# A fused attention, gated-convolution MLP and Fourier-mixing kernel: two of batch 0's eight MLP units in split numbers, eight opening products of zeros, another planner setting and order

## Chip, cores and metric

The kernel runs on one core of one Trainium2 chip. The metric is the device time of one execution in microseconds. The kernel before took 733.38 us (median of 3 runs, 733.23 to 734.42); the execution whose trace is read here took 731.59 us.

## What is computed

```python
# q, k, v: (4 batches, 8 heads, 576 tokens, 64); d_model 512
def _attn_ref(q, k, v):            # heads 0-3: window of 32; heads 4-7: window 128, every 4th token
    scores = np.where(masks[None], scale * (q @ k.T), -1e9)
    attn = softmax(scores)
    return attn @ v
def _moe_ref(x, w_in, conv_w, w_out):          # 512 -> 1024 -> 512
    h = np.maximum(x @ w_in, 0.0)
    gate = sigmoid(conv3(h, conv_w))           # along the tokens
    return (h * gate) @ w_out
def _moe2_ref(x, w_ch1, w_ch2):                # 512 -> 2048 -> 512
    u = x + real(fft(fft(x, axis=1), axis=2))
    un = layernorm(u)
    return u + np.maximum(un @ w_ch1, 0.0) @ w_ch2
```

The three weight matrices arrive as 64-bit floats and are turned into 32-bit numbers on the chip.

## The kernel before

**Numbers.** Most products are made with split numbers: an fp32 value is cut into a high part (rounded by writing it as fp32r) and a low part (value minus high part), and `mm3` (L291) issues three fp32r products, high by high, high by low and low by high. A plain `mm` on fp32 operands is one product that the trace shows as two matmul records.

**Stages.** (1) Attention: 14 steps a batch (`tick`, L648), each with score products, a maximum over partitions on GpSimd, an exponential on ScalarE, value products and transposes. The result of a batch is its tokens, transposed: for batch 0 in plain fp32 (`x_first`, L552), for the others split (`x_even` for batch 2, `x_odd` for 1 and 3). (2) The gated MLP, eight units of 128 hidden columns a batch (`mlp1`, L1395): `m1` (L738) makes a unit's hidden columns in two halves of 290 tokens, four products over d_model each, then the convolution and gate on ScalarE and VectorE; `m2` (L773) multiplies by the second matrix with `mm3`. (3) The Fourier transform as products with tables. (4) Layer norm and the second MLP in sets of 6 token tiles; there the first product uses seven products of 256-column blocks in place of eight (`weights7`, `sums7`, `tokens7`, L1175 to L1218, make the block sums on VectorE).

**Weights of the first MLP.** `Weights.convert` (L573) loads a raw 64-bit block, and `narrow` (L599) makes fp32 of it in three VectorE operations. For the second matrix `split` (L586) copies the high part and subtracts for the low part. For the first matrix the split is put off: batch 0 uses the plain fp32 weight. `narrow` writes it to one of three buffers (`ways`), a DMA copies it into its place, batch 0's `m1` multiplies it with `x_first` by plain `mm`, and `W1.later(f)` (L591, called for batch 1 at L1400) makes the split there: a copy for the high part and a subtraction that overwrites the plain weight.

**Order.** Nothing is issued in the order in which it is written. Every operation is a `Work` with estimated costs on the engines that can do it, a due time and its dependencies. `Plan.order` (L318) simulates the engines with these costs and always takes the most urgent ready work; the result is a fixed instruction stream for each engine. A transfer is planned to land 2.0 us after its bytes have gone over the bus (L408). Before that, each entry of `NUDGES` (L193) is a random seed that shifts the due times in one stretch of the plan by up to 8 us. Where the plan finds TensorE idle for over 0.4 us it fills the gap with small products (`busy_with`, L1301).

**Opening.** TensorE begins with 11 products of zeros (L1321) while the first operands arrive. The first transfers (L1337 to L1344) go over two queues, SP's and ScalarE's; the mask's middle part, `maskt[:, 384:768]`, is the last of them, on SP. `tick` 0 needs the mask's first part, `tick` 1 the middle part, and the dilated ticks the last part.

Of the kernel before, what the change touches and what calls it, by code (L numbers as in the profile page):

```python
# [45 lines left out]
T0 = 42.0  # L46
ROOT = (False, True, True)
PER = 68.0
T4 = T0 + 4 * PER
WHEN = {"dft": ((T4 - 65, 3.4), (T4 - 31, 3.4), (T4 + 40, 2.0), (T4 + 65, 2.5)), "first": (T4 - 2, 5.4),  # L50
        "rest": T4 + 44, "lead": 8.0, "six": 15.5}
# [136 lines left out]
class Work:  # L188
# [1 line left out]

NUDGES = (72935, 65452, 92148, 75732, 27922, 34960, 38538, 92972, 84579, 18235, 76564, 47731,  # L193
          74478, 2462, 75030, 82671, 84525, 15307, 83166, 68938, 50299, 5828, 74961, 19298,
          26748, 40657, 30353, 18642, 13928, 90295, 84765, 10537,)


LAT = {"PE": 0.25, "DVE": 0.12, "ACT": 0.15, "POOL": 0.2, "SP": 0.0, "NO": 0.0}
# [5 lines left out]
class Plan:  # L204
# [113 lines left out]
    def order(self):  # L318
        W = self.works
        for w in W:  # L320
            w.succ, w.left, w.ready, w.start = [], len(w.deps), 0.0, None
        for w in W:
            for d in w.deps:
                W[d].succ.append(w.id)
        self.urgency()
        for seed in NUDGES:
            rng = random.Random(seed)
            a = rng.uniform(0, 560)
            z = a + rng.uniform(4, 50)
            amp = rng.choice((1, 2, 4, 8))  # L330
            for w in W:
                if a < w.key < z:
                    w.key += rng.uniform(-amp, amp)
        self.urgency()
        free = dict.fromkeys(("PE", "DVE", "ACT", "POOL", "SP", "NO"), 0.0)
        can = {e: {} for e in free}
        bus, drift, last = 0.0, 0.0, 0.0
        out = []
        seen = dict.fromkeys(self.uses, (0, 0.0))

        def fill(t0, t1):


            free_at = []
            for tile_, uses in self.uses.items():
                i, end = seen[tile_]
                while i < len(uses) and uses[i][0].start is not None:
                    x = uses[i][0]
                    i, end = i + 1, max(end, x.start + x.where[x.eng])
                seen[tile_] = i, end  # L350
                if 0 < i < len(uses) and uses[i][1]:
                    free_at.append((end, len(free_at), tile_))
            end, _, tile_ = min(free_at, default=(t1, 0, None))
            n = int((t1 - max(t0, end) - 0.25) / 0.12)
            return self.busy_with(tile_, max(t0, end), n) if n > 0 else []

        def can_wait(w, end):
            return w.key < 1e8 and end < w.key + min(w.where.values()) + drift

        def offer(w):  # L360
            for e in w.where:
                can[e][w.id] = w
        for w in W:
            if not w.left:
                offer(w)
        while any(can.values()):
            best = None
            for e, c in can.items():
                if c:
                    t = max(free[e], min(w.ready for w in c.values()))  # L370
                    if best is None or t < best[0]:
                        best = t, e
            t, e = best
            pick = None

            wait = WAIT.get(e, 0.0)
            for w in sorted((w for w in can[e].values() if w.ready <= t + wait + 1e-9), key=lambda w: w.key):
                late = False
                for e2, us in w.where.items():
                    if e2 != e:  # L380
                        queue = sum(x.where[e2] for x in can[e2].values()
                                    if x.key < w.key and x.ready <= t and len(x.where) == 1)
                        if max(free[e2], t) + queue + us < t + w.where[e] - 1e-9 and not (
                                us < w.where[e] and can_wait(w, t + w.where[e] + 0.5)):
                            late = True
                if not late:
                    pick = w
                    break
            if pick is None:

                free[e] = min([f for x, f in free.items() if f > t + 1e-9] + [t + 0.3])
                continue
            w = pick
            for x in w.where:
                del can[x][w.id]
            t = max(t, w.ready)
            w.start, w.eng = t, e
            if e == "PE":
                if 8.0 < t and t - last > 0.4 and self.busy_with:
                    out += fill(last, t)  # L400
                last = t + w.where[e]
                drift += 0.1 * (t - w.key - drift)
            end = t + w.where[e]
            free[e] = end
            if w.bytes:
                begin = max(bus, end)
                bus = begin + w.bytes / (300e3 if begin < 60.0 else 280e3)
                end = bus + 2.0  # L408
            out.append(w)
            for s in w.succ:  # L410
                x = W[s]
                lat = 0.0 if w.bytes else LAT[e] if e not in x.where else 0.0
                x.ready = max(x.ready, end + lat)
                x.left -= 1
                if not x.left:
                    offer(x)
        assert all(w.start is not None for w in W), [w.id for w in W if w.start is None][:5]
        return out
# [51 lines left out]
def tile_kernel(ctx: ExitStack, tc: tile.TileContext, forms, qt_in, qt_first, ktp, ktd, vtp, vtd, wm1, wm2, conv_w,  # L470
# [22 lines left out]
    def dve(op_, us, key=None, **kw):  # L493
        P.run({"DVE": us}, op_, key, **kw)
# [68 lines left out]
    class Weights:  # L563
# [9 lines left out]
        def convert(self, where, raw, load=True):  # L573
            _, i, f = self.todo[self.at]
            self.at += 1
            w = self.tiles[i, f] = where
            if load:
                dma(raw, self.src[f, :, i])
            if self.late and not i:
                way = ways()  # L580
                self.narrow(raw, way)
                dma(w[:, 0].bitcast(F32), way)
            else:
                self.split(w, raw)
# [153 lines left out]
    def m1(b, f, h_banks, at):  # L738
# [8 lines left out]
        for half in range(2):  # L747
            o = of("h", h_banks)[:, :HS + 2]
            sl = slice(286 * half, 286 * half + HS + 2)
            with P.products(at + 4.3 * half):  # L750
                for c in range(4):
                    wsl = slice(128 * c, 128 * c + 128)
                    if b:
                        mm3(o, w[:, 0, wsl], w[:, 1, wsl], xT[b][:, c, 0, sl], xT[b][:, c, 1, sl], c == 0, c == 3)
                    else:
                        mm(o, w[:, 0, wsl].bitcast(F32), x_first[:, c, sl], c == 0, c == 3)
            P.run({"ACT": 0.41}, "activation", out=hp[:, HW + 2:] if half else hp[:, 1:HW],
                  in_=o[:, HS + 1:0:-1] if half else o, func=AF.Relu, scale=0.5)
# [416 lines left out]
    def weights7(j, raw, stage):  # L1175
# [8 lines left out]
        s1, s2, s3, s4 = (o[:, k] for o in odd for k in (k0, k1))  # L1184
        for o, a, b, op in ((s1, x[1][:, k0], x[1][:, k1], ALU.add), (s2, s1, x[0][:, k0], ALU.subtract),
                            (s3, x[0][:, k0], x[1][:, k0], ALU.subtract), (s4, x[0][:, k1], s2, ALU.subtract)):
            dve("tensor_tensor", on_dve(256), out=o, in0=a, in1=b, op=op)
        for k, a in ((0, x[0]), (2, x[1][:, k1]), (3, odd[0]), (5, odd[1])):
            n = a.n() // 256
            o, a = stage[:, k:k + n], a.rearrange("p (i n) -> p i n", i=n)  # L1190
# [10 lines left out]
    def sums7(j, raw, place_):  # L1201
# [6 lines left out]
        x21, x22, s3, s4 = (b[:, 256 * i:256 * i + 256] for i in range(4))  # L1208
        for o, x, y, op in ((s1, x21, x22, ALU.add), (s2, s1, x11, ALU.subtract),
                            (s3, x11, x21, ALU.subtract), (s4, x12, s2, ALU.subtract)):  # L1210
            dve("tensor_tensor", on_dve(256), out=o, in0=x, in1=y, op=op)
        for i, r in enumerate((a, b)):
            o = place_[:, 2 * i:2 * i + 2]
            v = r[:, 512:1024].rearrange("p (i n) -> p i n", i=2)
# [3 lines left out]
    def tokens7(s, place7):  # L1218
# [6 lines left out]
                load_un(place7[name][:, :, :, 128 * i:128 * i + 128], k, cs)  # L1225

        def tt(o, a, b, op=ALU.subtract):
            dve("tensor_tensor", on_dve(o.n()), out=o, in0=a, in1=b, op=op)

        def split(v, a):  # L1230
            copy(v[:, 0], a, ("ACT", "POOL"))
# [86 lines left out]
    dve("memset", 0.3, key=-98, out=idle)  # L1318
    zeros = idle.bitcast(BF16)[:, 0:512]
    with P.products(-97):  # L1320
        for _ in range(11):  # L1321
            mm(bank[7], zeros[:, 0:128], zeros, True, True)
    P.run({"POOL": 7.0}, "partition_all_reduce", out_ap=tiny, in_ap=tiny, channels=32,
          reduce_op=bass_isa.ReduceOp.max, key=-100)
# [13 lines left out]
    first(KT[0][:, 0:224], ktp[0, :, 0:224])  # L1338
    first(ident16, ident16_in, "ACT")
    first(QT[0][:, :, 0:192], qt_first)  # L1340
    first(KT[0][:, 224:608], ktp[0, :, 224:608])
    for h, queue in ((0, "SP"), (1, "ACT")):
        first(QT[0][h:128:2, h, 192:], qt_in[0, h, :, 192:], queue)
    first(maskt[:, 384:768], mask[:, 384:768])  # L1344
    P.key = loads[0] + 1
    kq_load(1)
    P.key += 1
# [47 lines left out]
    def mlp1(b, f0, f1, h_banks):  # L1395
        step = PER / NF1
        for f in range(f0, f1):
            at = T0 + PER * b + step * f
            if b == 1:
                W1.later(f)  # L1400
            m1(b, f, h_banks, at)
            m2(b, f, at + 2 * step)

# [207 lines left out]
```

## Time and profile before

| | |
|---|---|
| median of 3 runs | 733.38 us |
| profiled execution | 731.59 us |
| its span, first to last instruction | 729.7 us |
| TensorE matmul busy | 720.5 us |
| TensorE weight loads busy | 634.8 us |
| VectorE busy | 550.3 us |
| ScalarE busy | 341.8 us |
| GpSimd busy | 163.4 us |

Times in the rows below are microseconds from the span's start. PE is TensorE's matmuls, PEld its weight loads, DVE VectorE, ACT ScalarE, POOL GpSimd, SPq and ACTq the issue of DMAs on SyncE's and ScalarE's queues. A name such as `pb<-y,wf` is output from inputs: `pb` a PSUM bank, `wf` a weight place, `y` the storage in which `x_first` lies, `x` split tokens, `hid` the gated hidden values, `sm` an attention tile. A matmul's own duration holds its latency, which overlaps with the next; what a product costs is the distance from its start to the next one's.

### The profile page before, as it was taken

To read this page: it belongs to the slowest core of one execution; us is meant where nothing else is said; L and a number is where in the kernel's file an instruction comes from. 1 tells how busy PE (TensorE), PEld (TensorE's weight loads), DVE (VectorE), ACT (ScalarE), POOL (GpSimd) and SP (SyncE) were. 2 spreads that over 40 slices of the span, in tenths; PEclk is the share of its full clock that TensorE was granted. 3 is DMA by queue.
4 is the path that set the end of the run, shared out by engine and by line. 5 is a ranking of instruction groups with operands and counts; after the bars stand their busy time and mean duration, and the time that the engine had idled before them with its cause. 6 is when DMAs were issued, how large, how long until landed. Compare 5 with 4: busy or idle time off the path is not lost.

```text
span 729.7 us, 11759 instructions
## 1 busy us (share of the span) xinstructions
PE 720.5 (99%) x4135; PEld 634.8 (87%) x4135; DVE 550.3 (75%) x1119; ACT 341.8 (47%) x882; POOL 163.4 (22%) x181
## 2 busy tenths in 40 slices
PE   8999999999999999999999999999999999999998
PEld 6888889998998999888888788898888898888896
DVE  5999999899988689989886986776788548224223
ACT  4877767665876654663343424332233314222211
POOL 6845546353465123201100000000100000000000
PEclk9999999999999999999999999999999999999999
DMA  8967535115321836688877642045467799447202
GB/s 269 322 198 220 184 118 168 57 59 179 104 82 29 316 117 202 198 285 284 275 254 240 198 107 67 30 144 156 119 216 251 294 360 331 119 116 239 79 1 87
DMA packets 76750, 129.02 MB, mean 177 GB/s; under 512 B 7754, under 2 KB 36810, under 8 KB 76052
## 3 DMA queue, kind: packets, MB, share of 16 engines
q1 hardware_dynamic: 75892, 125.37, 53.2%
q0 software_dynamic: 432, 2.67, 1.0%
q8 instruction: 33, 0.54, 0.3%
q10 hardware_dynamic: 368, 0.23, 0.1%
q14 instruction: 25, 0.20, 0.1%
HBM read 90.21 MB, written 35.94 MB: 173 GB/s over the span
## 4 chain that ended last, share of the span: by engine, by line
PE 84%; DVE 7%; DMA 5%; POOL 1%; ACT 1%; SPq 1%; issue 1%; DVEq 0%; POOLq 0%; ACTq 0%
PE pb L274 84%; DVE rows L261 2%; DVE win L261 1%; DMA raw<-in_wm_dram 1%; DVE sm L261 1%; DMA work<-ud 1%; DMA maskt<-in_mask_dram 1%; SPq L307 1%; DVE work L261 1%; DMA wf<-y 1%; POOL mx L261 1%; DMA yd<-y 1%; DMA x<-nd 0%; DVE raw L261 0%; DVE hid L261 0%
## 5 line engine op out<-in xcount | busy, mean ns | idle before, releaser
L274 PE MATMUL pb<-wf,hid 128*128 128x512 f32 x870 | 230.6, 399 | 0.1
L274 PEld LDWEIGHTS pb<-wf,hid 128*128 128x128 f32 x870 | 157.1, 188 | 26.5 <-DVE hid L261 0.7
L261 POOL PARTITION_ALL_REDUCE mx<-sm x56 | 82.9, 1504 | 50.2 <-DVE sm L261 26.4
L274 PE MATMUL pb<-wf,wc 128*128 128x384 f32 (+1 forms) x414 | 85.6, 343 | 0.5 <-DVE work L261 0.5
L274 PE MATMUL pb<-x,wf 128*128 128x290 f32 x576 | 85.7, 300 | 0.0
L274 PEld LDWEIGHTS pb<-x,wf 128*128 128x128 f32 x576 | 80.4, 189 | 1.8
L274 PEld LDWEIGHTS pb<-wf,wc 128*128 128x128 f32 x414 | 74.1, 188 | 6.8 <-DVE work L261 0.8
L261 DVE TENSOR_TENSOR work<-pb,work 128x384 f32<-128x384 f32 x48 | 26.7, 556 | 66.7 <-ACT work L261 35.0
L261 DVE SCALAR_TENSOR_TENSOR rows<-rows,convw 128x578 f32<-128x578 f32 x64 | 57.6, 900 | 2.4 <-ACT rows L261 1.6
L261 ACT COPY work<-pb 128x384 f32<-128x384 f32 x48 | 23.0, 479 | 77.5 <-PE pb L274 77.5
L274 PE MATMUL pb<-wf 128*128 128x512 f32 x216 | 55.3, 393 | 0.0
L274 PEld LDWEIGHTS pb<-wf 128*128 128x128 f32 x216 | 40.1, 188 | 6.5
L274 PEld LDWEIGHTS pb<-VT,sm 104*72 104x72 f32 (+1 forms) x448 | 40.0, 153 | 4.8 <-ACT sm L261 1.2
L274 PE MATMUL pb<-VT,sm 104*72 104x65 f32 (+1 forms) x448 | 41.2, 235 | 1.3 <-ACT sm L261 0.7
L691 ACT ACTIVATE xb<-pb,rs 72x64 f32<-72x64 f32 (+1 forms) x176 | 39.7, 305 | 5.4 <-DVE rs L261 5.0
L274 PE MATMUL pb<-QT,KT 128*104 128x144 f32 (+1 forms) x224 | 40.9, 305 | 0.0
L274 PE MATMUL pb<-wf,wf 128*128 128x512 f32 (+1 forms) x162 | 39.8, 386 | 0.0
L261 ACT ACTIVATE rows<-pb 128x290 f32<-128x290 f32 (+1 forms) x64 | 26.3, 413 | 21.9 <-PE pb L274 21.6
L274 PEld LDWEIGHTS pb<-QT,KT 128*104 128x104 f32 (+1 forms) x224 | 33.4, 178 | 3.3 <-issue 1.2
L261 ACT ACTIVATE hid<-pb 128x512 fp32r<-128x512 f32 (+1 forms) x32 | 18.2, 570 | 36.4 <-PE pb L274 36.4
L274 PEld LDWEIGHTS pb<-wf,wf 128*128 128x128 f32 x162 | 30.0, 188 | 6.0 <-ACT y L261 0.4
L274 PE MATMUL pb<-y,wf 128*128 128x290 f32 x128 | 34.3, 410 | 0.0
(198 smaller groups left out, 1279.8 us busy)
## 6 DMA issues: line engine op xcount, KB each, us to landing
raw<-in_wm_dram SPq DMA_DIRECT2D x42, 512.0 KB, 4.6
wc<-cd SPq DMA_DIRECT2D x56, 256.0 KB, 3.4
cd<-wc SPq DMA_DIRECT2D x4, 1792.0 KB, 10.3
rows<-ud SPq DMA_DIRECT2D x20, 256.0 KB, 3.0
yd<-y SPq DMA_DIRECT2D x18, 256.0 KB, 4.4
y<-yd SPq DMA_DIRECT2D x18, 256.0 KB, 4.6
ud<-y SPq DMA_DIRECT2D x18, 256.0 KB, 4.2
wf<-nd SPq DMA_DIRECT2D x18, 256.0 KB, 6.1
```

The lines of the kernel that those rows point to most:

```text
L261: getattr(self.engines[eng], name)(**a)
L274: getattr(self.engines["PE"], name)(*[v.real() for v in a], **kw)
L307: self.engines[eng].dma_start(out=out.real() if outs else out, in_=in_.real() if ins else in_)
L691: nc.scalar.mul(out=x[:, i], in_=p[:, i], mul=r[:, i:i + 1])
```

## The change

- `WHOLE = 6`: the units 6 and 7 of the first matrix are split when they are converted (`split`, in place, no `ways` buffer, no DMA copy), and their `W1.later` in batch 1 goes. Batch 0's `m1` for these two units uses `mm3`, and before unit 6 its tokens are split into `x_even`: four copies and four subtractions of 128x576.
- 8 products of zeros in place of 11.
- The mask's middle part is issued earlier, on ScalarE's queue, ahead of the rest of the first keys.
- The plan's numbers: a transfer that begins after 200 us lands 3.5 us after its bytes rather than 2.0; the block sums cost 1.2 times and the token sums 1.1 times as much as before.
- `NUDGES`: 27 of the 32 seeds stay, 26 are new, so the order of the whole kernel is another.

```diff
+WHOLE = 6
+SURE = 200.0
-NUDGES = (72935, 65452, ..., 84765, 10537,)                    # 32 seeds
+NUDGES = (72935, 65452, ..., 46324, 2076,)                     # 53 seeds
...
-                end = bus + 2.0
+                end = bus + (2.0 if begin < SURE else 3.5)
...
-            if self.late and not i:
+            if self.late and not i and f < WHOLE:
                 way = ways()
                 self.narrow(raw, way)
                 dma(w[:, 0].bitcast(F32), way)
...
-                    if b:
+                    if b or f >= WHOLE:
                         mm3(o, w[:, 0, wsl], w[:, 1, wsl], xT[b][:, c, 0, sl], xT[b][:, c, 1, sl], c == 0, c == 3)
                     else:
                         mm(o, w[:, 0, wsl].bitcast(F32), x_first[:, c, sl], c == 0, c == 3)
...
-            dve("tensor_tensor", on_dve(256), out=o, in0=a, in1=b, op=op)
+            dve("tensor_tensor", 1.2 * on_dve(256), out=o, in0=a, in1=b, op=op)
...
-            dve("tensor_tensor", on_dve(o.n()), out=o, in0=a, in1=b, op=op)
+            dve("tensor_tensor", 1.1 * on_dve(o.n()), out=o, in0=a, in1=b, op=op)
...
-        for _ in range(11):
+        for _ in range(8):
             mm(bank[7], zeros[:, 0:128], zeros, True, True)
...
     first(QT[0][:, :, 0:192], qt_first)
+    first(maskt[:, 384:768], mask[:, 384:768], "ACT")
     first(KT[0][:, 224:608], ktp[0, :, 224:608])
     for h, queue in ((0, "SP"), (1, "ACT")):
         first(QT[0][h:128:2, h, 192:], qt_in[0, h, :, 192:], queue)
-    first(maskt[:, 384:768], mask[:, 384:768])
...
-            if b == 1:
+            if b == 1 and f < WHOLE:
                 W1.later(f)
+            if b == 0 and f == WHOLE:
+                for c in range(4):
+                    copy(x_even[:, c, 0], x_first[:, c], ("ACT", "POOL"))
+                    lo_of(x_even[:, c, 1], x_first[:, c], x_even[:, c, 0])
```

## Rows read from the trace of the kernel before

**Rows 1.** The page's first part: each engine's busy time, share of span, instructions.

```profile
PE 720.5 (99%) x4135; PEld 634.8 (87%) x4135; DVE 550.3 (75%) x1119; ACT 341.8 (47%) x882; POOL 163.4 (22%) x181
```

**Rows 2.** Waits of PE over the whole span: total, times, longest.

```profile
PE pb L274 <- DMA maskt<-in_mask_dram: 1.1, 2, 0.6
PE pb L274 <- ACT work L261: 0.8, 1, 0.8
PE pb L274 <- ACT sm L261: 0.7, 1, 0.7
PE pb L274 <- DVE work L261: 0.5, 1, 0.5
PE pb L274 <- ACT rs L261: 0.5, 1, 0.5
```

**Rows 3.** Busy time by stretch: length, then each engine's, clock, DMA share, GB/s.

```profile
41.00:100.00 59.00, 58.10 (x342) 47.74 (x341) 57.76 (x102) 42.91 (x134) 30.55 (x32) 1.00 0.58 184
100.00:150.00 50.00, 50.00 (x364) 46.71 (x363) 45.81 (x86) 35.46 (x110) 26.32 (x29) 1.00 0.35 106
...
200.00:250.00 50.00, 49.67 (x352) 45.53 (x351) 40.04 (x79) 34.58 (x106) 23.89 (x27) 1.00 0.41 138
```

**Rows 4.** Timeline of PE, batches 0 and 1: start, length, work, count.

```profile
40.14 2.14 PE L274 MATMUL pb<-y,wf 128*128 128x290 f32 x8
42.12 0.81 PE L274 MATMUL pb<-VT,sm 128*96 128x65 f32 x8
...
83.27 2.12 PE L274 MATMUL pb<-y,wf 128*128 128x290 f32 x8
...
97.77 2.17 PE L274 MATMUL pb<-y,wf 128*128 128x290 f32 x8
...
113.15 1.90 PE L274 MATMUL pb<-x,wf 128*128 128x290 f32 x12
114.89 0.34 PE L274 MATMUL pb<-ident,xb 96*128 96x96 f32 x2
```

**Rows 5.** Timeline of all engines and queues, the first 16 us.

```profile
0.73 0.41 ACTq L307 DMA_DIRECT2D maskt<-in_mask_dram  x1
...
1.37 4.78 PE L274 MATMUL pb<-sm 128*128 128x512 bf16 x11 [1.37 <-DVE sm L254]
...
5.98 0.33 PE L274 MATMUL pb<-maskt,ident 128*128 128x384 bf16 x1
...
7.53 0.32 PE L274 MATMUL pb<-maskt,ident 128*128 128x384 bf16 x1 [0.57 <-DMA maskt<-in_mask_dram]
...
8.81 0.43 SPq L307 DMA_DIRECT2D maskt<-in_mask_dram  x1
...
9.23 7.04 POOL L261 PARTITION_ALL_REDUCE mx<-sm  x5 [0.22 <-ACT sm L261]
```

**Rows 6.** The chain that ended last, in order of time: two transfers after 200 us.

```profile
393.15 5.78 DMA work<-ud
...
532.67 6.48 DMA raw<-in_wm_dram
```

**Rows 7.** Instruction groups by shape, PE: the plan's filling products.

```profile
L1309 PE MATMUL pb<-ident 128*128 128x256 bf16 x10 | 1.4, 274 | 0.0
```

**Rows 8.** Timeline of DVE, POOL and PE between 80 and 107 us.

```profile
80.68 0.69 DVE L261 TENSOR_TENSOR wf<-raw,wf 128x512 fp32r<-128x512 f32 x1
...
86.77 0.76 DVE L261 TENSOR_TENSOR hid<-rows,hid 128x576 fp32r<-128x576 f32 x1 [0.56 <-POOL hid L261]
...
94.12 1.92 POOL L261 PARTITION_ALL_REDUCE mx<-sm  x1
94.68 1.31 DVE L261 TENSOR_TENSOR wf<-raw,wf 128x512 fp32r<-128x512 f32 x1
...
96.12 0.53 PE L274 MATMUL pb<-wf,hid 128*128 128x512 f32 x1
...
106.27 0.36 DVE L261 TENSOR_TENSOR x<-pb,x 128x192 fp32r<-128x192 f32 x1 [0.45 <-ACT x L261]
```

More of the change, by code (lines that the diff above doesn't have):

```diff
@@ L189 @@
     __slots__ = ("where", "fn", "deps", "key", "bytes", "after", "start", "eng", "left", "ready", "succ", "id")
-NUDGES = (72935, 65452, 92148, 75732, 27922, 34960, 38538, 92972, 84579, 18235, 76564, 47731,
-          74478, 2462, 75030, 82671, 84525, 15307, 83166, 68938, 50299, 5828, 74961, 19298,
-          26748, 40657, 30353, 18642, 13928, 90295, 84765, 10537,)
+NUDGES = (72935, 65452, 92148, 75732, 27922, 34960, 38538, 84579, 92863, 47731, 74478, 2462,
[4 rows of a table added]
 LAT = {"PE": 0.25, "DVE": 0.12, "ACT": 0.15, "POOL": 0.2, "SP": 0.0, "NO": 0.0}
@@ L1210, in sums7 @@
                             (s3, x11, x21, ALU.subtract), (s4, x12, s2, ALU.subtract)):
-            dve("tensor_tensor", on_dve(256), out=o, in0=x, in1=y, op=op)
+            dve("tensor_tensor", 1.2 * on_dve(256), out=o, in0=x, in1=y, op=op)
         for i, r in enumerate((a, b)):
```

4 rows, old and new, of the table NUDGES are left out of this document.

## The prediction

> **What bounds the kernel now.** I read first the engines' busy time [rows 1], then who PE waits for [rows 2], then the busy time by stretch [rows 3], and last the timelines of the places that the change touches [rows 4, 5, 8] and the chain of waits [rows 6].
>
> PE is busy for 720.5 of 729.7 us [rows 1]. The reader should see in that line how little is to be had: of the 9.2 us without a product, 1.4 lie before the first one [rows 5], 4.1 are five kinds of waits that add up to 1.1 + 0.8 + 0.7 + 0.5 + 0.5 plus a few of 0.5 and less [rows 2], and the 3.7 that are left lie outside these rows. So only three things can shorten the kernel: less work on PE, an earlier first useful product, and fewer waits. One more place is hidden in "busy": the plan itself put ten small products into gaps, 1.4 us of busy time with nothing to compute [rows 7].
>
> The second thing to see is DVE. Over the whole span it is at 75%, which looks harmless, but that average mixes stretches: from 41 to 100 us, while batch 0 runs through its MLP, DVE is busy for 57.76 of 59 us, from 100 to 150 for 45.81 of 50, and only after 200 does it have a fifth of its time free [rows 3]. In that first stretch two engines are full at once, so whatever is added to DVE there matters.
>
> **The change part by part.**
>
> *Units 6 and 7 by split numbers: PE.* One half of a unit in plain fp32 (four products, eight records) starts at 40.14, and what follows starts at 42.12: 1.98 us. The same half in split numbers (twelve products) takes from 113.15 to 114.89: 1.74 us [rows 4]. Two units have four halves, so 4 x 0.24 = 0.96 us less on an engine with no slack. I take -1.0, with 0.1 us a half for the neighbour that comes after: -0.6 to -1.4. All of it counts, since PE does nothing else meanwhile.
>
> The Trainium skill, page "FP8 and Floating Point Precision", section TensorE Precision Notes, says that true fp32 makes four passes through the array. Three passes in place of four would save a quarter of 1.98, or 2.0 us in all as an estimate from that page; the rows show about half of it, and the rows decide.
>
> *The same units: DVE, ACT, POOL, DMA.* The split of batch 0's tokens adds four subtractions of 128x576, as the one that makes `hid`: 0.76 us each [rows 8], 3.0 us. It also adds four copies of that size on ACT or POOL, which are busy for 42.91 and 30.55 of 59 us there [rows 3] and hide them. The two weight subtractions are moved, not added: from batch 1 to before unit 6, 0.69 us each [rows 8], 1.4 us. So by the time unit 6 starts, at 83.27, and unit 7 ends, near 100 [rows 4], DVE has 4.4 us more to do, and 1.24 us were idle there. Two DMA issues on SP and their copies go, and with them the way through a buffer; neither SP nor the transfers hold anything there (DMA share 0.58 [rows 3]), so I cost that at nothing. If DVE can't be relieved the price is several microseconds: the low part of one weight is written from 94.68 to 95.99 and the product that reads it starts at 96.12 [rows 8], no margin at all. What relieves it: copies out of PSUM and the scaling of attention results which the planner may give to DVE or to ACT, the room on DVE after 100 us, and the 1 us that the opening moves everything forward. I take +0.4, between 0 and 4.4.
>
> *A new wait.* `x_even` was free until batch 2 wrote it; now batch 2's writes wait for batch 0's last product. That ends near 99.8 (97.77 + 2.0 [rows 4]) and the first low part of batch 2 is written at 106.27 [rows 8]. Behind it on ACT and DVE would stand the batch-1 work; with 6 us of distance it costs nothing.
>
> *The opening.* The eleven products of zeros begin at 1.37 and the first useful product starts at 5.98, right behind the last of them, with no wait of its own [rows 5]. They are 4.61/11 = 0.42 us apart, so eight end 1.26 us earlier. The useful product then starts when its operands are there, which no row shows; it is between 4.7 and 5.98. The second step waits until 7.53 for the mask's middle part, 0.57 us [rows 5], and that is the transfer which is moved ahead. On ACT's queue it costs one issue of 0.41 us [rows 5] before a part of the first queries; on SP the later transfers get one issue earlier, among them the mask's last part, whose issue at 8.81 [rows 5] is followed by the other half of the 1.1 us of waits for masks [rows 2]. From 9.23 on, POOL makes five reductions in 7.04 us without a break [rows 5], so the opening is worth what it moves POOL's first reduction. I take -0.8; ends 0 (the operands come just before 5.98) and -1.3.
>
> *Longer transfers in the plan, dearer sums.* The two long waits after 200 us follow late transfers: one of 256 KB took 5.78 us and one of 512 KB 6.48 [rows 6], where the old plan reckons, by its own figures (0.42 us an issue, 280 KB a us), issue, bytes and 2.0 us: 0.4 + 0.9 + 2.0 = 3.3 and 0.4 + 1.9 + 2.0 = 4.3. The new one says 4.8 and 5.8, so most of the shortfall is gone and loads come earlier or their users later. The waits behind them are the 0.8 for ACT's `work` and the 0.5 for DVE's `work` [rows 2]. I take -1.0; ends 0 and -1.3.
>
> *The new order.* No row of before shows it. Its nearest rows are the waits in the middle, 0.7 + 0.5 + 0.5 [rows 2], and the filling products, 1.4 [rows 7]: 3.1 us that another order can remove, or make anew. I take -0.5, a small part of it, since the order has to fit the fuller DVE as well; ends -3.1 and +3.1.
>
> *Sum.* -1.0 + 0.4 - 0.8 - 1.0 - 0.5 = -2.9 us. Against the profiled execution that is 731.6 - 2.9 = 728.7. That execution was 1.8 us below the median of the runs, so for the median I forecast 733.4 - 2.9 = **730.5 us**. A measurement of this kernel can tell about 0.2%, 1.5 us, from no change.
>
> **The rivals.**
>
> *Slower: DVE becomes the bound of batch 0.* The 4.4 us go in front of units 6 and 7 and only the 1.24 idle us take any of it. Then products of unit 6 and 7 start 3.2 us late, PE has nothing to put there, and since it is full afterwards it never gets the time back. With this PE's waits grow by 3.2, the transfers' waits stay half (-0.5) and the opening is lost, because DVE is what it would have fed: 733.4 + 3.2 - 1.0 - 0.5 = 735.1. For it: 57.76 of 59 us and the margin of 0.13 us. Against it: flexible copies, and POOL and ACT with room. It decides when more than about 3 us of the 4.4 can't be put elsewhere.
> A mechanism that makes this dearer: the subtraction that takes 0.69 us at 80.68 takes 1.31 at 94.68, under a POOL reduction from 94.12 to 96.04 [rows 8]. If all six subtractions meet a reduction they take 7.9 us in place of 4.4, and the sum above becomes 738.6. The Trainium skill, page "SBUF — State Buffer", section Who interferes with whom, has that rule: a DVE instruction with two SBUF inputs contends with a GpSimd instruction that reads SBUF. By that rule the new subtractions pay whenever POOL works, and the trace agrees with its 1.31. Chance of this rival with both prices: 0.10.
>
> *No measurable change: the order gives it back.* The products saved and the opening come (-1.8), the transfers' waits turn up elsewhere, and the new order has 1.2 us more waits: 732.8. For it: each order has some 4 us of waits, whatever it was planned with. Chance 0.16.
>
> *The clock.* The zeros pass 512 columns in 0.42 us [rows 5], 1.2 a nanosecond, the pace of the lower of TensorE's two levels (1.2 GHz); later the split half passes 12 x 290 columns in 1.74 us, 2.0 a nanosecond [rows 4], which only the upper level (2.4 GHz) allows. Before it rose the engine did nothing but the eleven zeros, one behind the other. After eight it may stand idle until its operands come, and the rise can come later. The first steps' products then take twice as long, while POOL takes 1.4 us for each reduction [rows 5] and hides most of it: by my estimate from these rows up to +0.4 for each of five steps in place of the opening's -0.8, so 730.5 + 0.8 + 2.0 = 733.3. Chance 0.05.
>
> *Much faster: the order clears nearly all.* The upper ends: -1.4, -1.3, -1.3, -2.5 and no price on DVE: -6.5, 726.9. Chance 0.15.
>
> **How the numbers follow.** The forecast, between 729.0 and 731.8, has 0.54. Faster by over 0.2% are the forecast and the much faster case: 0.69. Within 0.2%: order and clock, 0.21, of which 0.02 may fall on the slow side. Slower: 0.10 plus 0.02, so 0.12, 0.19 and 0.69. The range reaches to the much faster case below and to the slow rival's first price above: 727.0 to 735.0; it leaves out the slow rival under POOL and half of the much faster case.
>
> **What would show it.** Right: records of plain fp32 halves fall from 128 to 96 and 48 split ones appear before batch 1; the first mask product near 5.2 and the second near 6.5; no PE wait over 0.5 us near 400 and 540; DVE still near 98% up to 100 us with PE at 98% or more. Wrong: PE waits for DVE's `hid`, `wf` or `x` between 80 and 120; batch 0's last half starting later than the 97.77 of before [rows 4]; more of the filling products than ten; score products at double spacing behind the zeros.

## The result, and the profile after

The changed kernel takes 739.07 us (median of 4 runs, 738.81 to 740.42) against 733.73 us before in the same comparison: 5.3 us slower by the medians. The ratio, taken over all runs, is 1.0079 (5.8 us), 95% interval 1.0063 to 1.0094. Faster had been forecast.

The page's first part, the changed kernel (each engine's busy time, share of the span, instructions):

```profile
PE 729.3 (99%) x4214; PEld 642.6 (87%) x4214; DVE 558.5 (76%) x1122; ACT 342.1 (46%) x879; POOL 166.0 (22%) x195
```

The span is 738.4 us. PE is still at 99%, so the share says nothing: against [rows 1] it is busy for 8.8 us *more*, though the split units need less of it. The instruction groups of PE by shape say with what:

```profile
L278 PE MATMUL pb<-y,wf 128*128 128x290 f32 x96 | 26.0, 413 | 0.0
L278 PE MATMUL pb<-x,wf 128*128 128x290 f32 x624 | 93.8, 300 | 0.1
L1313 PE MATMUL pb<-ident 128*128 128x256 bf16 x76 | 9.6, 273 | 0.0
```

The first two lines are the change as written: 32 records of plain fp32 went, 48 split products came. The third answers to [rows 7]: 76 filling products in place of 10. They compute nothing; each is a place where the plan itself had no work for PE. The 66 more of them are 8.2 of the 8.8 us. PE's waits, answering to [rows 2] (total, times, longest):

```profile
PE pb L278 <- ACT sm L265: 1.8, 3, 0.7
PE pb L278 <- DVE sm L258: 1.4, 1, 1.4
PE pb L278 <- DVE sm L265: 0.8, 2, 0.5
PE pb L278 <- DMA QT<-in_qt_first_dram: 0.7, 1, 0.7
```

The waits after 200 us, for `work` on ACT and DVE, and those for the masks are gone, as forecast. In their place stand holes after 200 us which the fillers hide from this view. The timeline of PE around the first large hole (start, length, work, count):

```profile
88.18 1.93 PE L278 MATMUL pb<-x,wf 128*128 128x290 f32 x12
89.94 0.87 PE L278 MATMUL pb<-wf,hid 128*128 128x512 f32 x3
...
91.53 1.76 PE L278 MATMUL pb<-x,wf 128*128 128x290 f32 x12
93.13 0.68 PE L278 MATMUL pb<-VT,sm 104*72 104x65 f32 x8
...
95.66 2.79 PE L1313 MATMUL pb<-ident 128*128 128x256 bf16 x24
98.29 0.29 PE L278 MATMUL pb<-ident,xb 72*128 72x72 f32 x2
98.38 1.87 PE L278 MATMUL pb<-x,wf 128*128 128x290 f32 x12
...
100.78 1.90 PE L278 MATMUL pb<-x,wf 128*128 128x290 f32 x12
102.52 1.55 PE L278 MATMUL pb<-wf,hid 128*128 128x512 f32 x6
```

The four split halves of batch 0 take 1.76, 1.60, 1.71 and 1.74 us to the next start, 6.8 together. Before, the four halves from 83.27 to 97.77 took 1.74, 1.95, 2.01 and 1.78, 7.5 together. So the step saves 0.7 us where 0.96 had been worked out from one pair. Between the second and the third half PE passes 2.6 us on 24 fillers, and the last half starts at 100.78 in place of 97.77. DVE is as full there as before, 58.09 of 59 us (busy time by stretch, answering to [rows 3]):

```profile
41.00:100.00 59.00, 58.59 (x370) 48.54 (x369) 58.09 (x104) 43.41 (x136) 30.40 (x33) 1.00 0.53 167
100.00:150.00 50.00, 49.12 (x345) 45.07 (x345) 46.40 (x84) 34.05 (x102) 24.28 (x28) 1.00 0.38 117
```

Two of the four added subtractions stand in this stretch, in front of the hole (DVE):

```profile
75.40 0.74 DVE L265 TENSOR_TENSOR x<-y,x 128x576 fp32r<-128x576 f32 x1
...
87.44 0.74 DVE L265 TENSOR_TENSOR x<-y,x 128x576 fp32r<-128x576 f32 x1
```

The other two start at 40.72 and 43.46. All four took 0.72 to 0.75 us, so none paid the dearer price of 1.31 that the forecast named for a subtraction under a POOL reduction.

A second hole, 30 fillers, lies between 344.6 and 348.3, among the layer norms of the Fourier stage. Where the distance between the two kernels arises is read from the same work in both traces. Groups of instructions by tile, PE: count, durations in ns, first and last start. Before:

```profile
L274 PE MATMUL pb<-y,wf x128: 405/407/463, 33.7 to 99.5; 128*128 128x290 f32 x128
L274 PE MATMUL pb<-VT,sm x448: 218/228/297, 11.6 to 231.6; 104*72 104x65 f32 x86, 128*96 128x65 f32 x64
L274 PE MATMUL pb<-ident,y x32: 270/272/327, 277.5 to 342.7; 128*128 128x128 f32 x32
L274 PE MATMUL pb<-wf,wc x414: 333/334/440, 475.0 to 716.2; 128*128 128x384 f32 x120, 128*128 128x512 f32 x18
```

After:

```profile
L278 PE MATMUL pb<-y,wf x96: 406/407/512, 35.9 to 82.9; 128*128 128x290 f32 x96
L278 PE MATMUL pb<-VT,sm x448: 219/228/298, 12.5 to 236.6; 104*72 104x65 f32 x86, 128*96 128x65 f32 x64
L278 PE MATMUL pb<-ident,y x32: 270/272/274, 285.4 to 351.4; 128*128 128x128 f32 x32
L278 PE MATMUL pb<-wf,wc x414: 333/334/398, 484.5 to 724.7; 128*128 128x384 f32 x120, 128*128 128x512 f32 x18
```

The first MLP half starts 2.2 us later, the last attention product 5.0, the last transposes of the Fourier stage 8.7, and the last product of the second MLP 8.5. So the distance is made before about 350 us, in several places. Behind that nothing is lost or won on balance, though 9 fillers stand at 417.7 us where before had its two waits for `work`. (The trace shows 8.7 us where the medians show 5.3: the profiled execution of before was 2.1 us under its median and that of after 1.4 over.)

In the opening the useful products follow the zeros at half pace. All engines, the changed kernel:

```profile
1.39 3.60 PE L278 MATMUL pb<-sm 128*128 128x512 bf16 x8 [1.39 <-DVE sm L258]
...
4.77 0.53 PE L278 MATMUL pb<-maskt,ident 128*128 128x384 bf16 x1
...
5.95 1.62 PE L278 MATMUL pb<-QT,KT 128*128 128x192 f32 x4 [0.65 <-DMA QT<-in_qt_first_dram]
...
11.87 0.81 PE L278 MATMUL pb<-QT,KT 128*128 128x192 f32 x4
```

Four score products take 1.62 us at 5.95 and 0.81 at 11.87. The granted clock reads 1.00 at both places, so the half pace is read from these durations alone. The first mask product comes at 4.77, earlier than forecast, but the second at 7.36 in place of 6.5, and POOL's first reduction at 8.18 against 7.56 before. So three signs that the forecast had named for its own failure stand in this trace: more fillers than ten, double spacing behind the zeros, and a later last half of batch 0. The runs below tell which of them costs the time.

### The profile page after: what moved, and what is told of

Read it like the earlier page. It is cut to its first block, busy times and chain, and to the rows that moved or that the text cites. A ratio compares the mean times of both kernels' runs of the same rounds, so it can differ in the third digit from the quotient of the medians.

```text
span 738.4 us, 11917 instructions
## 1 busy us (share of the span) xinstructions
PE 729.3 (99%) x4214; PEld 642.6 (87%) x4214; DVE 558.5 (76%) x1122; ACT 342.1 (46%) x879; POOL 166.0 (22%) x195
## 4 chain that ended last, share of the span: by engine, by line
PE 83%; DVE 12%; DMA 1%; issue 1%; POOL 1%; ACT 1%; SPq 0%; DVEq 0%; ACTq 0%
PE pb L278 82%; DVE win L265 3%; DVE rows L265 3%; DVE sm L265 2%; DVE raw L265 1%; DVE x L265 1%; DVE hid L265 1%; DMA raw<-in_wm_dram 1%; DVE wf L265 1%; PE pb L1313 1%; POOL mx L265 1%; DMA QT<-in_qt_first_dram 1%; DVE y L265 0%; DVE xb L692 0%; ACT rows L265 0%
## 5 line engine op out<-in xcount | busy, mean ns | idle before, releaser
L278 PE MATMUL pb<-wf,hid 128*128 128x512 f32 x870 | 227.9, 398 | 0.2 <-DVE hid L265 0.2
L278 PE MATMUL pb<-x,wf 128*128 128x290 f32 x624 | 93.8, 300 | 0.1
L278 PEld LDWEIGHTS pb<-x,wf 128*128 128x128 f32 x624 | 87.5, 189 | 2.6 <-ACT rows L265 0.4
L695 ACT ACTIVATE xb<-pb,rs 72x64 f32<-72x64 f32 (+1 forms) x184 | 41.4, 305 | 5.1 <-DVE rs L265 5.0
L278 PE MATMUL pb<-QT,KT 128*104 128x144 f32 (+1 forms) x224 | 42.9, 315 | 0.7 <-DMA QT<-in_qt_first_dram 0.7
L265 POOL CAST wc<-raw 128x512 fp32r<-128x512 f32 (+1 forms) x9 | 6.5, 724 | 150.8 <-PE pb L278 79.5
L265 ACT ACTIVATE rows<-pb 128x290 f32<-128x290 f32 x64 | 26.5, 414 | 28.2 <-PE pb L278 27.7
L278 PE MATMUL pb<-unt,wc 128*128 128x384 f32 x168 | 33.1, 335 | 0.0
```

The source lines that it names most:

```text
L265: getattr(self.engines[eng], name)(**a)
L278: getattr(self.engines["PE"], name)(*[v.real() for v in a], **kw)
L695: nc.scalar.mul(out=x[:, i], in_=p[:, i], mul=r[:, i:i + 1])
```

## The experiments

"The plan's end" is the latest end that `Plan.order` reckons with its own costs before it issues anything: 723.6 us for the kernel before, 732.0 for the changed one. Ratios are to the kernel before, run beside each and taken over all runs, so they can differ from the quotient of the medians by about 0.001; 0.001 is 0.73 us.

**Theory A**: the order is at fault. The seeds are the result of a search over one plan, and for any other plan they are a shuffle. **Theory B**: the parts are at fault, DVE's added work above all, or the late clock.

### The seeds alone

```diff
 # the kernel before
-NUDGES = (72935, ..., 10537,)
+NUDGES = (72935, ..., 2076,)       # the 53 of the changed kernel
```

> The kernel before with nothing changed but the 53 seeds of the changed kernel. Theory A (the order is at fault: seeds were found for one plan and are a random shuffle for any other): the parts are those of before, yet the time rises by as much as the plan says its end moves, 723.6 to 733.3, so about 743 us, and the trace has about 40 filling products in place of 10. Theory B (the parts are at fault: DVE's added subtractions, the late clock): within 1.5 us of before, 732 to 735.

Measured: 739.2 us, ratio 1.009 (1.006 to 1.0119). Without one changed part the kernel is slower by about as much. Fillers, and PE's two largest waits behind the one that opens the span (those for masks end at 7.5 and 15.1 us):

```profile
L1311 PE MATMUL pb<-ident 128*128 128x256 bf16 x40 | 6.2, 274 | 0.0
...
PE pb L276 <- DMA maskt<-in_mask_dram: 2.3, 2, 1.3
PE pb L276 <- DVE x L263: 1.6, 2, 0.8
```

The time goes theory A's way, by 6.9 us rather than the 9 to 10 expected. But this order is neither kernel's: 40 fillers in place of 10 and 76, and none of the changed kernel's two large holes (26 of the 32 seeds of before are among the 53, one fewer than the section on the change says). So e1 shows what seeds cost on a plan for which they were not searched. It doesn't show what they cost the changed kernel, and that both lose about as much may be chance. The run that changes the changed kernel's own seeds is e10, below.

### No seeds, and the wrong seeds

```diff
 # the kernel before
-NUDGES = (72935, ..., 10537,)
+NUDGES = ()
```

> The kernel before without any seed: due times as written. The plan says its end moves from 723.6 to 736.1. If seeds are the order and the order is the time (theory A), 744 to 746 if the plan is taken at its word, 741 to 743 if the chip gives back as much of it as with the new seeds (plan +9.7, chip +6.9). If the seeds hardly matter: 732 to 734.

Measured: 746.55 us, ratio 1.0194 (1.0175 to 1.0214): 14 us, the upper value and a little over. This is what the seeds of before are worth. The like for the changed kernel was not run. Its plan, reckoned with `NUDGES = ()`, ends at 749.8 us, against 732.0 with the 53 seeds. So by the plan these are no shuffle for the changed kernel: they too come from a search, one that had further to go, as e10 shows.

```diff
 # the kernel before; seeds of before
+WHOLE = 6                          # the split units alone, as in the change
```

> The kernel before with the units 6 and 7 by split numbers alone and the seeds of before, which were found for another plan: the plan ends at 741.6 in place of 723.6, with 120 filling products. Theory A: the same part that cost 2.6 us with fitted seeds now costs 12 to 18 us, 745 to 751 us. If the part and not the fit makes the time: 735 to 737.

Measured: 749.76 us, ratio 1.0241 (1.0207 to 1.0276). One part, with seeds that fitted until then, costs 17 us, more than the kernel before loses without any seed, and the fillers rise to 120:

```profile
L1311 PE MATMUL pb<-ident 128*128 128x256 bf16 x120 | 15.5, 273 | 1.9 <-DVE x L263 1.9
```

### The parts with seeds fitted to them

Lists of seeds were tried on the plan alone, keeping what brought its end earlier.

```diff
 # e10: the changed kernel; e11: before with the split units alone;
 # e12: before; e13: the changed kernel with WHOLE = 8 (no split units)
-NUDGES = (...)
+NUDGES = (...)                     # fitted to this plan: ends 727.0, 724.6, 722.7, 724.9
```

> The changed kernel with all its parts and another list of seeds, found by trying lists until the plan's own end came earlier: 727.0 in place of 732.0. Over the five kernels so far the time stood 5.9 to 10.5 us above the plan's end, 8.1 in the mean. Theory A (the seeds lost the time, and others give it back): about 735, between 733 and 737.5. Rival (VectorE's added work loses it, whatever the order): 738 or more.

> The kernel before with the units 6 and 7 by split numbers alone (eleven zeros, the mask where it was, transfers and sums planned as before) and seeds found for it: the plan ends at 724.6, against 723.6 for before. With the 8.1 us between plan and time: 732.7, ratio 0.998 to 1.003: the split units, once the order is fitted to them, cost no more than 1 us. If VectorE's three microseconds can't be moved by any order: 735 to 737.

> The kernel before with all its parts and seeds fitted further: the plan ends at 722.7 in place of 723.6. By the plan 0.9 us faster than before, 731.5, ratio 0.9988; by the scatter of plan against time, which is 1 to 2 us, anything from 0.997 to 1.001. A candidate for the fastest version.

> The changed kernel without its main part (units 6 and 7 of batch 0 in plain fp32 as before; zeros, mask, planned transfers and sums as changed) and seeds fitted to that plan, which ends at 724.9. By the 8.1 us between plan and time 733.0. If the split units are what is left of the loss after fitting (the fitted changed kernel stood 1.5 us above before), this is 1 to 2 us faster than that one: 732.5 to 733.5, ratio to before 0.999 to 1.001. If fitting itself is what lacks: the same 734 to 735, ratio 1.002.

| | plan's end | median, us | ratio to before (95%) |
|---|---|---|---|
| the changed kernel | 732.0 | 739.07 | 1.0079 (1.0063 to 1.0094) |
| e10, all parts, fitted | 727.0 | 734.31 | 1.0020 (1.0008 to 1.0033) |
| e13, all but the units, fitted | 724.9 | 733.82 | 1.0025 (1.0008 to 1.0041) |
| e11, the units alone, fitted | 724.6 | 734.80 | 1.0035 (1.0017 to 1.0052) |
| e12, before, fitted further | 722.7 | 733.83 | 1.0012 (0.9995 to 1.0029) |

Other seeds and nothing else bring the changed kernel from 1.0079 to 1.0020, 4.3 of its 5.8 us, and its fillers from 76 to 46 (e10; then two of DVE's lines):

```profile
L1315 PE MATMUL pb<-ident 128*128 128x256 bf16 x46 | 6.0, 273 | 0.0
...
41.75 1.41 DVE L267 TENSOR_TENSOR x<-y,x 128x576 fp32r<-128x576 f32 x2
44.85 0.74 DVE L267 TENSOR_TENSOR x<-y,x 128x576 fp32r<-128x576 f32 x1
```

That is theory A's 735 and not B's 738. In this order all four added subtractions start between 35 and 45 us, and no filler stands near 96; 21 stand between 33 and 51 us. So this part doesn't bring the hole near 96 in every order.

The rest isn't settled. The 1.5 us that e10 still lacks (0.6 to 2.4) may be a part's price or want of a better order. The units alone stand 2.6 us above before (2.2 by the medians) where the plan said 1.0, which is midway between the two expectations; but with the other parts, runs with and without the units can't be told apart (1.0020 and 1.0025). And e12, 0.9 us better by the plan, is 0.9 us worse on the chip, inside its interval of no change. Plans that end 4.3 us apart (e12 and e10) measure 0.5 apart, so differences of this size in the plan's end don't order kernels; those of 5 us and more do in the runs here.

### The split units, one cost at a time, in the order of before

```diff
 # e5: the plan reckons as before, but the four halves of units 6 and 7 send
-                        mm(o, w[:, 0, wsl].bitcast(F32), x_first[:, c, sl], c == 0, c == 3)
+                        # three fp32r products for each, on another weight's high part
...
 # e6: behind narrow of unit 6
+                for c in range(4):
+                    nc.vector.tensor_tensor(out=x_even[:, c, 1], in0=x_first[:, c], in1=x_first[:, c], op=subtract)
...
 # e9: behind the last second7
+                for c in range(4):
+                    nc.vector.tensor_tensor(out=win, in0=high, in1=high, op=subtract)
```

> The kernel before with its order kept; only the four halves of batch 0's units 6 and 7 send twelve split products of 128x290 on another weight's high part, in place of four plain fp32 ones, so these two units' hidden columns are left out. The forecast's step says 4 x 0.24 = 0.96 us faster than before (between 0.6 and 1.4), a ratio of 0.9987. Rival: other engines set the pace there and the time stays, ratio 1.000.

Measured: 732.07 us, ratio 0.9995 (0.9984 to 1.0007), 0.4 us faster, between 1.2 faster and 0.5 slower. The saving of about 1 us lies inside the interval; so does none.

> The kernel before with its order kept; behind unit 6's weight conversion (near 77 us) four more VectorE subtractions of 128x576 are sent whose results nobody uses. They take 3.0 us of an engine that is idle for 1.2 of 59 us. The slow rival of the forecast (VectorE bounds batch 0) says 1.8 to 3.0 us slower, ratio 1.0025 to 1.004. If the products in reserve cover it: under 0.5 us.

Measured: 735.04 us, ratio 1.0044 (1.0027 to 1.0061): 3.2 us slower, 2.0 to 4.5 (2.6 by the medians). The four took 2.79 us, so as far as can be told they were passed on whole. DVE's line, then PE's wait between 76 and 100 us, then the stretch:

```profile
77.55 2.79 DVE L1414 TENSOR_TENSOR x<-y 128x576 fp32r<-128x576 f32 x4
...
PE pb L274 <- ACT xb L691: 2.1, 1, 2.1
...
41.00:100.00 59.00, 55.63 (x329) 45.57 (x328) 57.81 (x101) 41.50 (x132) 30.62 (x32) 1.00 0.56 178
```

PE loses 2.5 us against the 58.10 of [rows 3] while DVE's busy time there is the same 57.8: a full engine can't take more, it can only do it later. The wait is put down to ACT, which stood behind DVE's reciprocal.

> The kernel before with its order kept; four VectorE subtractions of 128x512 whose results nobody uses are sent near 495 us, behind the last weight conversion, where VectorE is busy for about 70% of the time. Beside the run with four such subtractions near 77 us (3.2 us slower) this tells where VectorE bounds. Theory (it bounds batch 0 only): under 0.7 us, ratio 1.000. Rival (the fixed order passes on any delay, wherever it is): 2 to 3 us slower, ratio 1.003 to 1.004.

Measured: 734.0 us, ratio 1.0022 (1.0010 to 1.0034), 1.6 us slower, 0.7 to 2.5: between the two. The four took 2.86 us, and one product waits for DVE behind them (PE's waits between 490 and 510 us):

```profile
PE pb L274 <- DVE work L261: 1.3, 1, 1.3
```

So at these two places the fixed order passed on about half of an unplanned delay where DVE is busy for 70% of the time, and about all of it where DVE is full.

### The opening

```diff
 # e2: the changed kernel, 11 zeros sent; e3: the kernel before, 8 sent
 #     (in both the plan reckons as it did)
 # e15: the kernel before with
-        for _ in range(11):
+        for _ in range(8):
 # and, in e15 and e16,
+    first(maskt[:, 384:768], mask[:, 384:768], "ACT")      # ahead of the rest of the first keys
```

> The changed kernel with its order kept to the last instruction, only that 11 products of zeros are sent in place of 8 (the plan still counts 8). If the late rise of the clock costs what the first trace shows (full speed at 9.9 us in place of 5.9; POOL's first reduction at 8.18 in place of 7.56), the time falls by 1 to 2.5 us, to 736.5 to 738, and the score products behind the zeros are 0.16 us apart again. If something later absorbs it: 739.1, no change.

Measured: 739.7 us, ratio 1.0094 (1.0068 to 1.012): no gain over the 1.0079 of the changed kernel. In its trace the scores are at full pace from the first on, and nothing of that reaches the end.

> The kernel before with its order kept, only that 8 products of zeros are sent in place of 11 (the plan still counts 11). The forecast's step said faster by up to 0.8 us, since the first useful product is no longer behind the zeros: 732.9. The clock rival says slower by 1 to 2.5 us, 734.7 to 736.2, with score products 0.32 us apart until about 10 us.

Measured: 732.53 us, ratio 1.0000 (0.9984 to 1.0015): neither. The zeros are not what the second step waits for:

```profile
4.45 0.33 PE L274 MATMUL pb<-maskt,ident 128*128 128x384 bf16 x1
...
7.50 0.47 PE L274 MATMUL pb<-maskt,ident 128*128 128x384 bf16 x1 [1.53 <-DMA maskt<-in_mask_dram]
7.76 1.57 PE L274 MATMUL pb<-QT,KT 128*128 128x192 f32 x4
```

The first mask product came 1.5 us earlier than in [rows 5], the second at the same 7.5, and after that wait of 1.53 us the scores were at half pace. The granted clock was 0.50 there (third column from the end):

```profile
8.00:10.70 2.70, 2.70 (x9) 2.39 (x9) 0.56 (x1) 0.48 (x1) 0.79 (x2) 0.50 0.96 315
```

> The kernel before with 8 products of zeros and the mask's middle part issued earlier on ScalarE's queue, nothing else; the rest of the order stays as it was. The forecast's step said -0.8 us (0 to -1.3): 731.9. By the run with 8 zeros alone, and by the changed kernel's late clock: no gain, ratio 0.999 to 1.002.

> The kernel before with the mask's middle part issued earlier, and 11 zeros. In the changed kernel with 11 zeros sent, the second mask product came at 6.6 us rather than 7.53 and POOL's fourth reduction at 11.5 rather than 12.0. If that is passed on: 0.4 to 0.5 us faster, ratio 0.9994, a candidate for the fastest version, at the edge of what can be measured. If a later load takes it back: ratio 1.000.

Measured: 731.9 us, ratio 0.9990 (0.9977 to 1.0003), and 731.58 us, ratio 0.9990 (0.9976 to 1.0004). Both are 0.7 us faster by the ratio, the size of the forecast's step, and neither interval excludes no change. (Both were planned anew: PE's order is that of before, but for the zeros; three VectorE instructions come earlier and two of GpSimd change places.) With the mask alone (e16), PE and POOL:

```profile
5.23 0.33 PE L276 MATMUL pb<-maskt,ident 128*128 128x384 bf16 x1
...
6.50 0.33 PE L276 MATMUL pb<-maskt,ident 128*128 128x384 bf16 x1
...
7.27 8.47 POOL L263 PARTITION_ALL_REDUCE mx<-sm  x6 [5.90 <-ACT sm L263]
```

The second mask product comes 1.0 us earlier and POOL's reductions run in one piece from 7.27. These two are the fastest medians here, but not faster than before by what can be told.

### Transfers planned shorter

```diff
 # the changed kernel
-SURE = 200.0
+SURE = 1e9
```

> The changed kernel with transfers planned at 2.0 us throughout. Its order differs from about 200 us on; the 27 filling products near 345 us should go. The forecast's step said longer planned transfers save 1 us: then this is slower than the changed kernel, about 740. If the longer planning itself makes the hole near 345: 1 to 3 us faster, 736 to 738. The plan's end moves by -0.8 only.

Measured: 739.51 us, ratio 1.0099 (1.0083 to 1.0115), beside 1.0079 in another comparison: no gain, and no clear loss. The fillers fall from 76 to 45: the 9 near 418 us go, and those near 345 give way to a wait in the same place (PE):

```profile
346.68 0.61 PE L278 MATMUL pb<-wf,x 128*128 128x512 f32 x2
350.12 2.60 PE L278 MATMUL pb<-wf,x 128*128 128x512 f32 x10 [2.83 <-DVE x L265]
```

So the longer planning doesn't make the hole near 345; it only knows of it.

### Without the filling products

```diff
 # the changed kernel, in fill
-            return self.busy_with(tile_, max(t0, end), n) if n > 0 else []
+            return []
```

> The changed kernel with its order kept but without the 76 filling products (they compute nothing). They take 76 x 0.109 = 8.3 us of TensorE. Theory A (the order has real holes, and the fillers only sit in them): at most 1.5 us faster, 737.5 to 739.1, with waits of 2 to 3 us on TensorE near 96 and 345 us in their place. Rival (the fillers themselves are the loss): 66 x 0.109 = 7.2 us faster, about 732. A third way: the clock falls in a hole without them, and the time rises above 740.

Measured: 741.53 us, ratio 1.0122 (1.0093 to 1.015): slower by 2 to 3 us than with them, the third way. PE between 343 and 353 us, then the stretches with the granted clock (the third column from the end):

```profile
346.52 0.65 PE L278 MATMUL pb<-ident,y 128*128 128x128 f32 x4 [1.81 <-ACT y L265]
...
348.56 4.14 PE L278 MATMUL pb<-wf,x 128*128 128x512 f32 x10 [0.92 <-DVE x L265]
...
343.00:349.00 6.00, 3.28 (x16) 2.18 (x15) 5.76 (x14) 3.10 (x6) 0.52 (x1) 1.00 1.02 313
349.00:352.50 3.50, 3.50 (x10) 2.65 (x9) 3.26 (x7) 1.01 (x2) 0.00 (x0) 0.51 0.93 299
```

The holes are real: the waits stand where the fillers stood (the one near 96 is 1.96 us, for ACT's `xb`). After 1.81 and 0.92 us of waiting with six products between, the granted clock was 0.51 from 349 to 352.5, and ten products took 4.1 us. In e8 the same group of ten took 2.6 us behind a wait of 2.83, at a granted clock of 1.00, so the wait alone doesn't decide it. Over the span the mean granted clock was 0.993 to 0.998 in the four executions without fillers and 0.999 to 1.000 in the four with them. That fits fillers which cost little and help to keep the upper level; which hole they guard isn't shown.

## Why the prediction was wrong

**The step that failed is the term "the new order".** It stood in the sum with -0.5 and ends of -3.1 and +3.1. With every part kept, other seeds take 4.3 us off the changed kernel (e10: 1.0020 in place of 1.0079), so the order costs about that beside one that can be had. The plan's own end had said +8.4, and between the two traces the 66 added fillers are 8.2 us of the 8.7. The bounds were taken from the waits and fillers of before, as the nearest rows. But those are the rows of an order that a search had already cleared (a further one, e12, brought its plan only 0.9 us): they bound what another order can take away, not what it can add. Runs show how much that is: 14 us without seeds (e7), 6.9 and 17 with seeds of another plan (e1, e14). The rival "the order gives it back" named the right place and priced it at 1.2 us more waits; no row of before bounds that figure from above.

**What stays open** is the last 1.5 us, which e10 doesn't give back.

**Units 6 and 7 on PE**, -1.0: 0.7 by the trace, a little under the size worked out from one pair of halves; by time it is 0.4, with 1.2 and none inside the interval (e5).

**Their load on DVE**, +0.4, ends 0 and 4.4. In the order of before, 2.79 us of it cost 3.2 (e6), so the slow rival's mechanism is real at that place. In the changed order the 2.6 us of fillers near 96 stand behind two of the subtractions, and e10, which has all four earlier, has no filler there, so the load doesn't cost that much in every order. The net cost in a searched order lies between nothing (e10 beside e13) and about 2.6 us (e11) and stays open. The rival's dearer price didn't come: the four subtractions took 0.72 to 0.75 us each.

**The opening**, -0.8: 0.7 measured in the order of before (e15), at the edge of no change. As far as that can be told it is the mask that brings it, not the zeros (e3: nothing; e16: 0.7). The step's yardstick, POOL's first reduction, failed: in the changed order it came 0.6 us later than before, and sending eleven zeros, which moved it from 8.18 to 7.37, gained nothing (e2).

**The clock rival** gave 733.3 for double spacing behind the zeros. The spacing came in this trace and in that of e10, but not always: with eight zeros the trace of e15 has full pace from the first scores, and that of e3 falls back after its wait. No time follows it that the runs can tell (e2, e3).

**Longer planned transfers**, -1.0: the two waits went, as said, and no time came with them: the changed kernel with short ones is as fast within the intervals (e8). The step counted a wait that leaves the list as time gained.

**The range**, 727.0 to 735.0, left 739.07 outside because the order's ends were too near, not because a rival was left out. (The much faster case also isn't the sum of the upper ends: it takes -2.5 for the order, whose own end was -3.1, and with that it is 726.3.)

## What to carry to other kernels

An order found by search belongs to the plan it was searched for. Seeds of another plan cost 7 and 17 us here (e1, e14), and a search that stopped early 4 (the changed kernel beside e10), against parts worth about 1 us each. So search the order as far for the changed kernel as for the one before until a part is judged, or hold the order and send the changed instructions in it, as e5 and e6 do. If a kernel plans itself, read what its plan says of its own end and of its holes first: it had +8.4 us for this change, where the argument from waits had -2.9.
A busy share of 99% can hold work that computes nothing; look for it by name and count.

## What had not been expected of the hardware

A wait of TensorE doesn't say by its length whether the granted clock falls behind it. Two of 1.81 and 0.92 us, with six products between them, were followed by 0.51 for 3.5 us (e4), and one of 1.53 us in the opening by 0.50 until 10.7 us (e3). But 2.83 us near 350 (e8), 2.06 near 81 (e6) and 1.96 near 98 (e4 itself) were followed by 1.00. What decides it no run here shows.

With filling products of 0.109 us each in the holes (24 in 2.6 us) the changed kernel's mean granted clock was 0.999 to 1.000 in its four executions; without them it was 0.993 to 0.998 in all four, and the time was 2 to 3 us longer. An added 2.86 us on VectorE cost 1.6 us even where that engine was 70% busy (e9).
